# Moving the first sequence's stores and first row loads to other queues in the opening of an FFT, mixing and FFN kernel

## The chip, the cores and the metric

The kernel runs on one core of a Trainium2 chip. The core has five engines with queues of their own: TensorE (PE: matmuls; PEld: its weight loads), VectorE (DVE), ScalarE (ACT), GpSimd (POOL) and SyncE (SP, which only issues transfers here). Transfers (DMAs) run on 16 DMA engines, which SP's, ACT's and POOL's queues feed. The metric is device microseconds of one execution; less is better.

## The reference

Eight sequences of 3008 rows with 256 columns in float32 go through a real FFT along the sequence, a complex 256 x 256 mixing with bias, a soft threshold of 0.01, the inverse FFT, and then, as 24064 tokens, through a gated feed-forward block of width 1536:

```python
X = np.fft.rfft(x, axis=1)
Yr = Xr @ w_r - Xi @ w_i + b_r
Yi = Xr @ w_i + Xi @ w_r + b_i
Yr = np.sign(Yr) * np.maximum(np.abs(Yr) - lam, 0.0)
Yi = np.sign(Yi) * np.maximum(np.abs(Yi) - lam, 0.0)
y = np.fft.irfft(Y, n=x.shape[1], axis=1)
...
gate = 1.0 / (1.0 + np.exp(-(x @ w_gate)))
val = x @ w_val
return (gate * val @ w_out).astype(np.float32)
```

## The kernel before

3008 is 47 x 64. The FFT of a sequence is made in two stages with a transposition through device memory between them. The **first stage** (47 points) works on "units": `load_a(b, h)` loads unit h of sequence b (96 partitions x 4 x 256 floats, 384 KB) into a tile xf, `fwd_a(b, h)` (L178) makes two float32 products with the table `fa_sb` (`product_a`, L173) and copies each from its bank of PSUM back into xf, the first with ACT and the second with DVE for the sequences 0 and 1 (L184). `store_a(b, h)` (L186) stores the unit to zd[b]. A sequence has eight units. The **second stage** (64 points) works in twelve steps q: `load_b(b, q)` (L227) reads rows of zd[b] into a tile zf (three buffers), each step needing something of all eight stores; `load_mf(q)` loads the step's table; `fwd_b(b, q)` (L232) makes the product pb, copies it to xsh with ACT, takes the rest xsl with DVE and negates halves with ACT. `mix4` (L285) is the mixing for sequence 0 with 24 matmuls (pm, L293) and the soft threshold on DVE; `inv_b` (L298) is the inverse 64-point product (pi, L305), with the table mi of `load_mi`; its copy vz is stored to vd by POOL's queue. PSUM has three banks for all this (`FFT_BANKS`), so a product waits until the bank of the product three before it is copied out.

The change lies in the opening (L853 to L920), which handles sequence 0 whole, with the first stage of sequence 1 put in between. Its order is written out by hand (`tc.manual_schedule()`): every engine takes its instructions in the order of the text. Ahead of it stand 13 warming matmuls on a zeroed tile (`keep_warm`, L827 to L832, WARM). Then SP issues nine loads (eight units of sequence 0, one of sequence 1), and for each unit of sequence 0 the products run, and SP stores the unit; units 1 to 3 of sequence 1 are loaded behind units 1, 3 and 4, and the mixing weights w_r and w_i (`load_mix`, L747) behind unit 2. Then SP issues the table of step 0, the rows of steps 0 and 1, the table of step 1, two biases (`load_bias4`), a part of the feed-forward weights (`load_part`, the tile raw, 512 KB) and the table of step 2. TensorE makes four early units of sequence 1 (EARLY), with `mix_weights` (L760; ACT and DVE) behind the second, and ten warming matmuls (WARM_Z). Then come the steps q: rows for q + 2, the table mi, two stores of sequence 1 in each of the steps 0 and 1, the products of `fwd_b` for step q, `mix4` for q - 1, `inv_b` for q - 2, and the conversion of feed-forward weights in between.

After the opening the rest of the FFTs runs between the matmuls of the feed-forward block, in an order fixed by weights; none of that is touched.

```python
for h in range(EARLY):
    fwd_a(1, h)
    if h == 1:
        wi_sb = mix_weights()
keep_warm(bank("warm"), zero[:, :P], zero, WARM_Z)
```

Of the kernel before, what the change touches and what calls it, by code (L numbers as in the profile page):

```python
# [19 lines left out]
R2, R1 = 47, 64  # L20
NK2 = 24
NQ = 2 * NK2
# [10 lines left out]

LAST_GAP, SIDE_GAP = 20, 3
PRE = 2
WARM = 13
WARM_Z, WARM_V = 10, 5
EARLY = 4
AT_FIRST = 3
NCONV = 7  # L40
# [69 lines left out]
def tile_fft_mix_ffn(ctx: ExitStack, tc, x, w_r, w_i, b_r, b_i, w_one, w_out, mf, mi, mis, fa, fb, out):  # L110
    nc = tc.nc
# [29 lines left out]
    def bank(name, tag="fft", bufs=FFT_BANKS):  # L141
        return (psf if tag == "fft" else psl).tile([P, 512], F32, tag=tag, bufs=bufs, name=name)
# [10 lines left out]
    zd = [tc.dram_tile([NQ, R1, D], F32, name=f"zd{b}") for b in range(B)]  # L153
# [12 lines left out]
    def big(name):  # L166
        return p2.tile([P, 4, D], F32, tag="big", bufs=NBIG, name=name)

    def load_a(b, h):
        xf = p0.tile([P, 4, D], F32, name="xf0", bufs=R1 // 8) if b == 0 else big("xf")  # L170
        nc.sync.dma_start(xf[:XR], xv[b, h])
        held["x", b, h] = xf

    def product_a(xi, az, copy):
        pa = bank("pa")[:2 * NQ]
        nc.tensor.matmul(pa, fa_sb, xi, start=True, stop=True)  # L176
        copy(az, pa.rearrange("p (h c) -> p h c", h=2))  # L177

    def fwd_a(b, h):

        xf = held["x", b, h]
        for i in range(2):
            at = slice(2 * i, 2 * i + 2)
            product_a(xf[:2 * R2, at], xf[:2 * NQ, at], nc.vector.tensor_copy if b < 2 and i else nc.scalar.copy)  # L184

    def store_a(b, h, queue=nc.sync):  # L186
        queue.dma_start(zv[b][:, 4 * h:4 * h + 4], held.pop(("x", b, h))[:2 * NQ])
# [14 lines left out]
    def load_mf(q):  # L202
        t = p2.tile([P, 2, P], F32, name="mf_sb", bufs=NMF)
        nc.sync.dma_start(t, mf[2 * q:2 * q + 2].rearrange("q p k -> p q k"))
        return t
# [18 lines left out]
        nc.gpsimd.dma_start(md[2 * q:2 * q + 2].rearrange("q p a k -> p q a k"), t.bitcast(F32))  # L224
        kept.add(q)

    def load_b(b, q):  # L227
        zf = p2.tile([P, 2, D], F32, tag="ld", bufs=NLD, name="zf")
        nc.sync.dma_start(zf, zd[b][4 * q:4 * q + 4].rearrange("(q a) n c -> (a n) q c", q=2))
        held["z", b, q] = zf  # L230

    def fwd_b(b, q, m, full):  # L232
        zf = held.pop(("z", b, q))
        pb = bank("pb").rearrange("p (c q k) -> p c q k", c=CT, q=2)
        for i in range(2):
            for ct in range(CT):
                nc.tensor.matmul(pb[:, ct, i], zf[:, i, ct * P:(ct + 1) * P], m[:, i], start=True, stop=True)  # L237
        xh, xl = (p2.tile([P, CT, 3, 2 * R1], F32R, tag=t, name=t) for t in ("xsh", "xsl"))
        if full:

            xh, xl = (t.rearrange("p c s k -> p c (s k)").rearrange("p c (q k) -> p c q k", q=2) for t in (xh, xl))
            nc.scalar.copy(xh[:, :, :, 64:], pb)
            sub(xl[:, :, :, 64:], pb, xh[:, :, :, 64:])
            for t in (xh, xl):
                nc.scalar.mul(t[:, :, :, :64], t[:, :, :, 128:], -1.0)
        else:

            xf = p2.tile([P, CT, 3, 2, R1], F32, name="xsf", bufs=1)
            nc.scalar.copy(xf[:, :, 0:2].rearrange("p c t q k -> p c q t k"),
                           pb.rearrange("p c q (t k) -> p c q t k", t=2))  # L250
            nc.vector.tensor_add(xf[:, :, 2], xf[:, :, 0], xf[:, :, 1])
            flat = xf.rearrange("p c s q k -> p c s (q k)")
            nc.scalar.copy(xh, flat)
            sub(xl, flat, xh)
        held["xs", b, q] = xh, xl
# [490 lines left out]
    def load_mix():  # L746
        for w in (w_r, w_i):  # L747
            wf = f2k("wf")
            nc.sync.dma_start(wf, w.rearrange("(t p) d -> p t d", p=P))
            wfs.append(wf)  # L750

    def load_bias4():
        for i, v in enumerate((b_r, b_i)):
            nc.sync.dma_start(bias4[64 * i:64 * i + 64], v.rearrange("(o d) -> o d", o=1).broadcast_to([64, D]))

    def load_bias():
        for i, v in enumerate((b_r, b_i)):
            nc.sync.dma_start(bias_sb[:, i], v.rearrange("(o d) -> o d", o=1).broadcast_to([P, D]))

    def mix_weights():  # L760
        wi = p0.tile([P, CT, 2, D], F32R, tag="xf0", bufs=R1 // 8, name="wi_sb")
        nc.scalar.copy(wi[:, :, 0], wfs[1])
        sub(wi[:, :, 1], wfs[1], wi[:, :, 0])
        wd, wn = f2k("wd"), f2k("wn")
        sub(wd, wfs[1], wfs[0])
        nc.vector.scalar_tensor_tensor(wn, wfs[0], -1.0, wfs[1], op0=ALU.mult, op1=ALU.subtract)
        for i, w in enumerate((wfs[0], wd, wn)):
            nc.scalar.copy(w_sb[:, :, 0, i], w)
            sub(w_sb[:, :, 1, i], w, w_sb[:, :, 0, i])
        return wi  # L770
# [24 lines left out]
    def load_part():  # L795
        k, f = parts.pop(0)
        if len(parts) >= 3 * NF // 2 - NCONV:
            raw = p0.tile([P, 2, D, 2], U32, tag="xf0", bufs=R1 // 8, name="raw0")
        else:
            raw = p2.tile([P, 2, D, 2], U32, tag="big", bufs=NBIG, name="raw")  # L800
        nc.sync.dma_start(raw.rearrange("p i n w -> p (i n w)"), (w_out[f // 2] if k else w_one[f]).bitcast(U32))
        raws.append((k, f, raw))
# [12 lines left out]
    def ops(names, i):  # L815

        for n in names.split() if -len(started) <= i < len(started) else ():
            started[i].pop(n)()
        if names.endswith("lo"):
            started[:] = [t for t in started if t]  # L820
# [6 lines left out]
    def keep_warm(o, l, r, n):  # L827

        for _ in range(n):
            nc.tensor.matmul(o, l, r, start=True, stop=True)  # L830

    keep_warm(bank("warm"), zero[:, :P], zero, WARM)  # L832
    tables = {}
# [5 lines left out]
    mfs, mis_ = {}, {}  # L839
# [13 lines left out]
    with tc.manual_schedule():  # L853
        for h in range(na):
            load_a(0, h)
        load_a(1, 0)
        for h in range(na):
            fwd_a(0, h)
            store_a(0, h)
            if h in (1, 3, 4):  # L860
                load_a(1, {1: 1, 3: 2, 4: 3}[h])
            if h == 2:
                load_mix()
        mfs[0] = load_mf(0)
        for q in range(2):
            load_b(0, q)
        mfs[1] = load_mf(1)
        load_bias4()
        load_part()
        mfs[2] = load_mf(2)  # L870
        for h in range(EARLY):
            fwd_a(1, h)
            if h == 1:
                wi_sb = mix_weights()
        keep_warm(bank("warm"), zero[:, :P], zero, WARM_Z)
        for q in range(NP + 2):
            if q + 2 < NP:
                load_b(0, q + 2)
            if 0 <= q - 1 < NP:
                mis_[q - 1] = load_mi(q - 1, True)  # L880
            if q < 2:
                for h in range(q * EARLY // 2, (q + 1) * EARLY // 2):
                    store_a(1, h)
            if q == 3:
                nc.sync.dma_start(fb_sb, fb)
                load_bias()
            if q % 2 and q <= NP:
                load_part()
            if q % 2 == 0 and 4 <= q < 4 + 2 * (na - EARLY):
                load_a(1, EARLY + q // 2 - 2)  # L890
            if q < NP:
                fwd_b(0, q, mfs[q], True)
            if q + 3 < NP:
                mfs[q + 3] = load_mf(q + 3)

            if q % 2:
                ops("sum word", 0)
                start_part(p0)
                ops("exp top", -1)
            elif q:  # L900
                ops("power mant", -1)
                if len(started) > 1:
                    ops("hi lo", 0)
                ops("one", -1)
            if q == 4:
                sub(bias_sb[:, 1], bias_sb[:, 1], bias_sb[:, 0])
            if 0 <= q - 1 < NP:
                mix4(0, q - 1)
            if q == NP + 1:

                fwd_a(1, EARLY)
                store_a(1, EARLY, nc.gpsimd)
            if 0 <= q - 2 < NP:
                inv_b(0, q - 2, mis_[q - 2], True)

        for bh in beside[:NR2K]:
            load_half(*bh)
        left = ["hi lo", "power mant one", "sum word", "hi lo"]
        for h in range(EARLY + 1, na):
            ops(left.pop(0), 0)  # L920
            fwd_a(1, h)
            store_a(1, h, nc.gpsimd)
        ops(left.pop(0), 0)
# [46 lines left out]
    n = len(a3) // 3  # L970
# [13 lines left out]
    for j in range(NF, len(ffn)):  # L984
        c, f = divmod(j, NF)
# [46 lines left out]
    with tc.manual_schedule():  # L1032
# [16 lines left out]
        n = NPR * NH  # L1049
# [36 lines left out]
```

## Time and profile before

| | us |
|---|---|
| median of 3 runs (2822.7 to 2823.41) | 2823.06 |
| the profiled execution's own time | 2821.45 |
| its span | 2819.6 |
| TensorE busy in the span (99%) | 2802.0 |
| VectorE busy (74%) | 2082.6 |
| ScalarE busy (46%) | 1309.8 |
| GpSimd busy (25%) | 711.7 |

The profile is of one execution. All places in it are microseconds from the start of the span. A line such as L237 is that of the program. "SPq", "ACTq" and "POOLq" are the queues in which those engines issue transfers; a transfer's time is from its issue to its landing. In rows of a timeline, x40 counts records (a float32 product leaves several), and the brackets tell how long the engine had been idle just before, and for what. MB are 10^6 bytes.

### The profile page before, as it was taken

The page shows a single profiled execution, that of the slowest core. Times are in us where ns is not written, and L with a number is a line of the kernel's source. Part 1 is how long each engine was busy: PE and PEld are TensorE (multiplying, and loading weights), DVE is VectorE, ACT ScalarE, POOL GpSimd, SP SyncE. Part 2 cuts the span into 40 slices and gives each one's busy share as a digit, 9 for nine tenths or more (in the row PEclk, how much of TensorE's full clock was granted, in tenths as well). Part 3 has the DMA queues.
Part 4 walks back from the last instruction along what each step waited for, and adds up shares of the span by engine and source line. Part 5 has one row for each costly group of instructions (what it writes and reads, how often), then busy time and mean ns, then how long its engine had stood idle before and what let it go on. Part 6 is the DMA issues. An engine that isn't in the chain of part 4 may idle for free.

```text
span 2819.6 us, 38247 instructions
## 1 busy us (share of the span) xinstructions
PE 2802.0 (99%) x13896; PEld 2307.9 (82%) x13896; DVE 2082.6 (74%) x3109; ACT 1309.8 (46%) x2276; POOL 711.7 (25%) x638
## 2 busy tenths in 40 slices
PE   9999999999999999999999999999999999999999
PEld 6778888888899887888888888888888888888887
DVE  5778778667787536777777777777777777777776
ACT  4664544544455444444444444444444444444443
POOL 0211010224100002333333333333333343333321
PEclk9999999999999999999999999999999999999999
DMA  9866545656554661000000000000000000000000
GB/s 295 265 214 190 172 138 156 200 180 191 163 156 144 185 182 36 30 15 16 30 31 24 7 31 31 31 16 15 31 30 16 15 30 31 30 1 30 30 16 16
DMA packets 173469, 241.01 MB, mean 85 GB/s; under 512 B 14592, under 2 KB 124896, under 8 KB 173280
## 3 DMA queue, kind: packets, MB, share of 16 engines
q1 hardware_dynamic: 163776, 214.93, 24.9%
q0 software_dynamic: 9408, 23.60, 2.5%
q8 instruction: 110, 1.80, 0.3%
q14 instruction: 79, 0.65, 0.1%
q10 hardware_dynamic: 96, 0.04, 0.0%
HBM read 134.17 MB, written 104.33 MB: 85 GB/s over the span
## 4 chain that ended last, share of the span: by engine, by line
PE 95%; DVE 2%; DMA 2%; ACT 0%; issue 0%; SPq 0%; DVEq 0%; ACTq 0%
PE pd L653 11%; PE pc L653 11%; PE pa L653 11%; PE po L630 8%; PE po L629 8%; PE po L628 8%; PE pm L271 6%; PE pb L653 5%; PE pia L340 4%; PE pa L176 3%; PE pb L237 3%; PE pg L395 2%; PE pg L397 2%; PE po L420 2%; PE pg L396 2%; PE po L421 2%
## 5 line engine op out<-in xcount | busy, mean ns | idle before, releaser
L630 PE MATMUL po<-hl,w 128*128 128x512 f32 x912 | 362.7, 398 | 0.0
L629 PE MATMUL po<-hh,w 128*128 128x512 f32 x912 | 361.7, 397 | 0.0
L628 PE MATMUL po<-hh,w 128*128 128x512 f32 x912 | 360.9, 396 | 0.0
L712 POOL TENSOR_TENSOR c<-c,c 128x512 f32<-128x512 f32 x114 | 147.7, 1296 | 833.5 <-DVE c L708 613.4
L653 PE MATMUL pc<-s,w1h 128*128 128x512 f32 x912 | 284.1, 393 | 1.4 <-DVE v L687 1.4
L653 PE MATMUL pa<-a,w1h 128*128 128x512 f32 x912 | 284.1, 393 | 0.0
L708 DVE TENSOR_TENSOR c<-u,pc 128x512 f32<-128x512 f32 x228 | 156.7, 687 | 114.7 <-PE pc L653 106.3
L683 DVE TENSOR_TENSOR u<-u,pb 128x512 f32<-128x512 f32 x228 | 155.3, 681 | 91.1 <-PE pb L653 64.1
L600 ACT CAST hh<-v 128x512 fp32r<-128x512 f32 x114 | 70.7, 620 | 306.0 <-DVE v L693 306.0
L630 PEld LDWEIGHTS po<-hl,w 128*128 128x128 f32 x912 | 171.5, 188 | 41.9
L628 PEld LDWEIGHTS po<-hh,w 128*128 128x128 f32 x912 | 172.1, 189 | 40.9
L629 PEld LDWEIGHTS po<-hh,w 128*128 128x128 f32 x912 | 171.1, 188 | 40.7
L653 PEld LDWEIGHTS pa<-a,w1h 128*128 128x128 f32 x912 | 171.2, 188 | 40.1
L653 PEld LDWEIGHTS pc<-s,w1h 128*128 128x128 f32 x912 | 170.9, 188 | 39.5 <-DVE v L687 2.3
L604 POOL TENSOR_TENSOR hl<-c,hh 128x512 fp32r<-128x512 f32 x114 | 152.6, 1338 | 186.1 <-ACT hh L600 186.1
L271 PE MATMUL pm<-w_sb,xsh 128*128 128x256 f32 x1008 | 189.4, 288 | 1.4 <-ACT xf L177 1.1
L653 PE MATMUL pc<-s,w1l 128*128 128x512 f32 x456 | 177.6, 389 | 0.0
L653 PE MATMUL pa<-a,w1l 128*128 128x512 f32 x456 | 177.0, 388 | 0.0
L685 DVE TENSOR_TENSOR v<-u,pd 128x512 f32<-128x512 f32 x228 | 156.8, 688 | 25.0 <-DVE u L683 0.9
L714 DVE TENSOR_TENSOR u<-u,pd 128x512 f32<-128x512 f32 x228 | 156.9, 688 | 24.4 <-DVE c L708 0.9
L687 DVE TENSOR_TENSOR v<-v,pc 128x512 f32<-128x512 f32 x228 | 156.6, 687 | 24.1 <-DVE v L685 0.5
L679 ACT COPY u<-pa 128x512 f32<-128x512 f32 x228 | 133.7, 586 | 81.6 <-PE pa L653 81.6
(166 smaller groups left out, 6739.6 us busy)
## 6 DMA issues: line engine op xcount, KB each, us to landing
zf<-zd SPq DMA_DIRECT2D x96, 256.0 KB, 3.5
vf<-vd SPq DMA_DIRECT2D x128, 192.0 KB, 3.2
out_dram<-ot SPq DMA_DIRECT2D x93, 256.0 KB, 2.2
vd<-vz SPq DMA_DIRECT2D x84, 256.0 KB, 2.9
ypair<-yd SPq DMA_DIRECT2D x19, 1024.0 KB, 5.0
yd<-yf SPq DMA_DIRECT2D x103, 188.0 KB, 3.1
xf<-in_x_dram SPq DMA_DIRECT2D x48, 384.0 KB, 4.2
zd<-xf SPq DMA_DIRECT2D x44, 384.0 KB, 3.6
```

The lines of the kernel that those rows point to most:

```text
L271: nc.tensor.matmul(o, l, r, start=(i == 0), stop=(i == len(mms) - 1))
L604: sub_(hl, h, hh)
L628: nc.tensor.matmul(o, wh, hh, start=(f == 0), stop=False)
L629: nc.tensor.matmul(o, wl, hh, start=False, stop=False)
L630: nc.tensor.matmul(o, wh, hl, start=False, stop=(f == NF - 1))
L653: nc.tensor.matmul(o, l, r, start=not more and l is wh and r is xh, stop=l is wl, skip_group_check=more)
L683: add(u, u, b)
L685: add(v, u, d)
L687: add(v, v, c)
L708: add(c12, u, c)
L712: nc.gpsimd.tensor_mul(c12, g12, c12)
L714: add(u, u, d)
```

## The change

The stores of sequence 0 are issued from ACT's queue in place of SP's. For sequence 0 the copies change places: DVE takes the first product of a unit, ACT the second. Units 2 and 3 of sequence 1 are loaded behind units 4 and 6 (before: 3 and 4); the table of step 0 is loaded behind unit 5 (before: after all units). The rows of the steps 0 and 1 are loaded from POOL's queue. Three early units of sequence 1 stay ahead of the second warming; the fourth is made behind the product of step 0. Stores of sequence 1 go out one in each of the steps 0 to 3. WARM falls from 13 to 10 and WARM_Z from 10 to 5.

```diff
-WARM = 13
-WARM_Z, WARM_V = 10, 5
+WARM = 10
+WARM_Z, WARM_V = 5, 5
...
-            product_a(xf[:2 * R2, at], xf[:2 * NQ, at], nc.vector.tensor_copy if b < 2 and i else nc.scalar.copy)
+            product_a(xf[:2 * R2, at], xf[:2 * NQ, at], nc.vector.tensor_copy if b < 2 and i == b else nc.scalar.copy)
...
-    def load_b(b, q):
+    def load_b(b, q, queue=nc.sync):
         zf = p2.tile([P, 2, D], F32, tag="ld", bufs=NLD, name="zf")
-        nc.sync.dma_start(zf, zd[b][4 * q:4 * q + 4].rearrange("(q a) n c -> (a n) q c", q=2))
+        queue.dma_start(zf, zd[b][4 * q:4 * q + 4].rearrange("(q a) n c -> (a n) q c", q=2))
...
             fwd_a(0, h)
-            store_a(0, h)
-            if h in (1, 3, 4):
-                load_a(1, {1: 1, 3: 2, 4: 3}[h])
+            store_a(0, h, nc.scalar)
+            if h in (1, 4, 6):
+                load_a(1, {1: 1, 4: 2, 6: 3}[h])
             if h == 2:
                 load_mix()
-        mfs[0] = load_mf(0)
+            if h == 5:
+                mfs[0] = load_mf(0)
         for q in range(2):
-            load_b(0, q)
+            load_b(0, q, nc.gpsimd)
         mfs[1] = load_mf(1)
         load_bias4()
         load_part()
         mfs[2] = load_mf(2)
-        for h in range(EARLY):
+        for h in range(EARLY - 1):
             fwd_a(1, h)
...
-            if q < 2:
-                for h in range(q * EARLY // 2, (q + 1) * EARLY // 2):
-                    store_a(1, h)
+            if q < EARLY:
+                store_a(1, q)
...
             if q < NP:
                 fwd_b(0, q, mfs[q], True)
+            if q == 0:
+                fwd_a(1, EARLY - 1)
```

## Rows read from the trace of the kernel before

**Rows 1.** Page, engines: busy us (share of the span) x instructions.
```profile
PE 2802.0 (99%) x13896; PEld 2307.9 (82%) x13896; DVE 2082.6 (74%) x3109; ACT 1309.8 (46%) x2276; POOL 711.7 (25%) x638
```

**Rows 2.** Windows: busy of PE, PEld, DVE, ACT, POOL; clock, DMA share, GB/s.
```profile
48.00:84.00 36.00, 36.00 (x281) 35.02 (x282) 31.40 (x55) 23.60 (x44) 5.82 (x8) 1.00 0.93 271
```

**Rows 3.** TensorE's waits, first 48 us: total us, times, longest.
```profile
PE pb L237 <- DMA zf<-zd: 1.5, 1, 1.5
...
PE pb L237 <- issue: 1.0, 1, 1.0
...
PE pb L237 <- DMA mf_sb<-in_mf_dram: 0.5, 1, 0.5
PE pi L305 <- DMA mi_sb<-in_mi_dram: 0.4, 1, 0.4
```

**Rows 4.** Timeline of TensorE: start, us, what, records, idle before.
```profile
6.28 17.49 PE L176 MATMUL pa<-xf,fa_sb 94*96 94x512 f32 x40
24.27 1.93 PE L176 MATMUL pa<-xf,fa_sb 94*96 94x512 f32 x4 [0.50 <-DMA xf<-in_x_dram]
...
28.10 2.77 PE L830 MATMUL warm<-zero 128*128 128x512 f32 x10
31.88 1.13 PE L237 MATMUL pb<-mf_sb,zf 128*128 128x128 f32 x8 [1.02 <-issue]
...
38.97 1.13 PE L237 MATMUL pb<-mf_sb,zf 128*128 128x128 f32 x8 [1.52 <-DMA zf<-zd]
```

**Rows 5.** Timeline of TensorE in two short stretches, three warming matmuls each.
```profile
2.90 1.48 PE L830 MATMUL warm<-zero 128*128 128x512 f32 x3
...
28.65 0.85 PE L830 MATMUL warm<-zero 128*128 128x512 f32 x3
```

**Rows 6.** Chain that ended last, first 60 us: start, us, what.
```profile
21.47 7.49 DMA zd<-xf
...
32.83 6.00 DMA zf<-zd
...
49.00 0.89 PE pb L237 x8
49.89 2.84 PE pm L293 x24
```

**Rows 7.** SP's waits, first 110 us: total us, times, longest.
```profile
SPq L171 <- DMA fa_sb<-in_fa_dram: 1.9, 1, 1.9
```

**Rows 8.** Timeline of SP's queue: issues of stores 3 and 4.
```profile
16.29 0.33 SPq L187 DMA_DIRECT2D zd<-xf  x1
...
17.95 0.31 SPq L187 DMA_DIRECT2D zd<-xf  x1
```

**Rows 9.** Timeline of ACT and of DVE: an issue, copies.
```profile
0.74 0.55 ACTq L151 DMA_DIRECT2D fa_sb<-in_fa_dram  x1
...
9.05 0.58 ACT L177 COPY xf<-pa 96x512 f32<-96x512 f32 x1 [1.14 <-PE pa L176]
...
8.19 0.69 DVE L177 COPY xf<-pa 96x512 f32<-96x512 f32 x1 [6.78 <-PE pa L176]
```

**Rows 10.** Transfers, first 60 us in 40 slices of 1.5 us.
```profile
GB/s 0 143 313 278 265 262 262 262 262 262 355 407 355 377 421 366 366 415 323 11 231 246 90 200 374 400 380 379 385 371 332 330 185 167 308 358 313 302 311 386
```

**Rows 11.** Issues from 5.5, 29.45, 44, 49 and 90 us: KB, us to landing.
```profile
xf<-in_x_dram SPq DMA_DIRECT2D x2, 384.0 KB, 10.7
...
zf<-zd SPq DMA_DIRECT2D x1, 256.0 KB, 3.1
...
vd<-vz POOLq DMA_DIRECT2D x1, 256.0 KB, 5.3
...
vd<-vz POOLq DMA_DIRECT2D x1, 256.0 KB, 7.7
...
vd<-vz POOLq DMA_DIRECT2D x1, 256.0 KB, 2.6
```

## The prediction

> **What bounds the kernel now.** I read the page first: TensorE is busy 2802.0 of 2819.6 us [rows 1], so only what TensorE waits for, or what is put there to fill a wait, can be won. Then the table by stretch: from 48 us to 84 us it is busy throughout, at a granted clock of 1.00 [rows 2], so whatever the first 48 us save moves all that follows. Then TensorE's waits: the larger ones of the opening are 1.5, 1.0, 0.5 and 0.4 us, all before the 64-point products of the first sequence (pb) or the inverse ones (pi) [rows 3]. Then its timeline: ten units of the first stage in one piece of 40 records from 6.28 us, one each 1.72 us (ACT's copy of 0.58 and its idle time of 1.14 [rows 9]), ten warming matmuls from 28.10, the first pb group at 31.88, the third at 38.97 [rows 4]. Last the chain: a store zd<-xf is on its way for 7.49 us and lands at 28.96, and a row load zf<-zd is on its way for 6.00 us to 38.83 [rows 6]. So the opening is bound by a round trip: the eighth store lands, then the rows are read back. Filler stands on TensorE because of that.
>
> All this lies within the first 40 of 2820 us. The runs' median, 2823.06, lies 1.61 above the profiled execution's own time of 2821.45 and 3.46 above its span. I take differences within the trace and set them against the median. 0.2% is 5.6 us, about what a measurement of this kernel can tell from no change.
>
> **Two facts about the queues, from rows.** SP's load issue waited 1.9 us for fa_sb, a transfer that ACT had issued [rows 7]. No data ties the two. fa_sb is the first hardware transfer and xf(0,7) the ninth: each transfer waits for the one eight before it, and both hardware queues share that count. Store 3 shows it: its copies are over about 14.0 us (8.88, the end of the first DVE copy [rows 9], and three units of 1.72), but SP issues it at 16.29 [rows 8], when xf(0,7), issued near 5.6 and 10.7 us on its way [rows 11], lands. Second, the rate: slices of 1.5 us show 262 GB/s while only loads flow, and 323 to 421 from 15 us on, with loads and stores mixed [rows 10].
>
> **WARM 13 to 10.** The first warming matmuls start 0.43 us apart (the 1.48 us of three, less the 0.62 of one, over two); those before the first pb 0.23 apart (0.85 less 0.39, over two) [rows 5]. The ratio is that of the two clock levels, 1.2 and 2.4 GHz. The three removed run at the end of the thirteen, mostly at the fast pitch: 3 x 0.23 = 0.7 us; at the slow one 1.3. I take 0.7, because the slow rows end near 5 us: units start at about 5.6. TensorE does not wait for this now, so by itself it only lets stores start earlier.
>
> **Stores of the first sequence on ACT's queue.** Per unit ACT gets one issue, 0.55 us [rows 9], beside one copy of 0.58; the idle time before a copy is 1.14, so it fits. With the copies swapped ACT makes the second one and issues behind itself; DVE's is done by then. Store 0 leaves about 0.9 us earlier. But stores keep their place in the count: store 3 waits for xf(0,7), now on ACT, store 4 for xf(1,0). Behind them in ACT stand the copies of units 4 and on; with three PSUM banks TensorE stalls some 1 to 2 us. That is paid before the round trip and not on it, so I cost it at nothing while TensorE is done before the rows arrive. Landing of the eighth store, from 28.95:
> - stores 0 to 2 flow beside loads from 9.5 to 15.5 us: at 380 GB/s (middle of the mixed slices) instead of 262, 0.71 MB more, 1.9 us at 380;
> - xf(1,3) and mf0 (0.39 + 0.13 MB) may land behind it, as they are in the other queue: 1.4 us at 380;
> - against it, mf1 and the short bias now go ahead of it (0.26 MB, 0.7 us), and part of raw: 0.4 us, estimated;
> - against it, while stores 3 and 4 wait on ACT, some 3 us fall back to 262: 0.35 MB, 0.9 us.
>
> Sum -1.3, so about 27.7. Ends: 28.95 and a little over if nothing overtakes (29.7 if half of raw, 0.26 MB, is ahead); 25.5 if neither of the last two items costs anything and mf1 and the bias stay behind.
>
> What speaks against: under load a single 256 KB store in POOL's queue took 5.3 to 7.7 us to land, 2.6 in a calm stretch [rows 11], so a queue of one's own is no free lane. The Trainium skill, "DMA: Bandwidth & Descriptors", section "Issuing engines are not separate DMA queues", says that DMAs of all engines share the same 16 DMA engines and that issuing from several saves only issue time. By that rule the landing stays at 28.95; it stands below as a rival.
>
> **Rows of steps 0 and 1 on POOL's queue.** Now the second zf takes 3.1 us on SP [rows 11], and the first pb starts 2.9 us after 28.96. A POOL transfer of this size, in the other direction, took 2.6 to 7.7 [rows 11]. In the calm state that I expect it is nearest to 2.6 to 3.1; the third step's rows and store (1,0), on SP, now share the engines: I take 3.5. POOL has nothing behind these two until its first vd store near 44.7. SP's own wait for the eighth store moves from zf 0 to zf 2; mf1, the biases, raw and mf2 pass it, so the 0.5 us wait for mf goes, and zf 2, issued at 32.83 now [rows 6], leaves right behind the eighth store. It was the largest wait, 1.5 us; it goes.
>
> **The fourth early unit behind the first pb; WARM_Z 10 to 5.** No work is added; 1.72 us move into the round trip's tail, where TensorE waited for mf and zf 2. Five warming matmuls less are 5 x 0.23 = 1.2 us. Its two copies fall behind xsh and xsl of step 0 on ACT and DVE, beside TensorE's next 0.89 us; nothing. The first pb is at T; then unit 1.72, pb 0.89, pm 2.84 [rows 6]. So the third pb is at T + 0.89 + 1.72 + 0.89 + 2.84 = T + 6.34, against 38.97. Break-even is T = 32.6.
>
> **The rest.** x(1,1) stays at its place, x(1,2) and x(1,3) come a unit or two later, but ahead of their use. Stores of the second sequence leave one per step: less to share early. Both cost nothing: no wait of rows 3 is theirs.
>
> **Sum.** T = 27.7 + 3.5 = 31.2; third pb at 37.5; 1.4 us won, and 0.1 of the 0.4 us pi wait, as mi is queued earlier. 2823.06 - 1.5 = **2821.6**. Its own range, with landing 27 to 28.5 and 3.1 to 3.8 us to the first pb: 2820.4 to 2822.6.
>
> **Rivals.**
> - *The transfers are the bound anyway*: ACT's stores wait for the same earlier transfers and the engines move the same bytes, so the change does not do what it says. Landing 28.95, T = 32.45, third pb 38.8: 0.2 won, **2822.9**. For it: the shared count, store 3. Against it: the 262 GB/s slices.
> - *The stores overtake*: landing 25.5, T = 29.0, third pb at 35.3, 3.6 won, and the 0.4 of pi: **2819.1**. For it: separate queues. Against it: the slow vd stores. The same page, "Queues, rings and completion order", has each DMA engine take turns between queues by packet, which would favour this; no run here shows two hardware queues busy together.
> - *Slower: the pair on POOL's queue lands late.* Place: TensorE's wait before the first pb. zf moves in short pieces beside the larger ones of raw and store (1,0); in the loaded stretch POOL's transfers took up to 7.7 us, middle 6.5. T = 34.2, third pb 40.5, 1.5 lost: **2824.6**. It decides once landing to pb exceeds 4.9 us (32.6 less 27.7). For it: the loaded rows. Against it: that stretch had eight transfers under way.
> - *Slower: TensorE's clock falls in the longer wait.* the third early unit needs x(1,2), for which TensorE waits until 24.27 now [rows 4]; with 1.72 and 1.2 of warming TensorE is done near 27.2 and idles to 31.2, nearly 4 us against 1.0 now [rows 3]. The ten slow matmuls at the start cost 10 x (0.43 - 0.23) = 2.0 us; 1.5 won less 2.0: **2823.6**. Against it: the clock held through 1.5 us of idling [rows 3], the longest I can show. The Trainium skill, "TensorE: Matmul & The Clock Gate", section "HAM oscillation — how this bites in real kernels", says waits for DMA between bursts can throttle the clock; no run here shows it.
>
> **How the numbers follow.** Forecast 0.42, bound anyway 0.20, overtaking 0.14, late pair 0.13, clock 0.11. 80% range: from just under overtaking to just over the late pair, 2818.9 to 2824.9; what is left out is a late pair together with a clock fall (2826.6), or a still larger gain. Faster by over 0.2% needs 5.6 us: all waits in rows 3 (3.4 us) and both shortened fillers (1.9) together give 5.3, so 0.02. Slower by over 0.2%: only if two mishaps add up, 0.03. Same: 0.95.
>
> **What would show it.** Stores 0 to 7 on ACT's queue, with ACT waiting some us before stores 3 and 4; the eighth landing near 27.7; rates over 300 in the slices from 9 to 15 us; the first pb near 31.2 after a wait of 3 to 4 us; the unit behind it; no wait before the second and third pb; pitches of the first records unchanged. I am wrong in the step on the stores if the landing stays at 29, in the step on POOL if zf takes over 4.9 us, and in the clock if the first pb records are twice as long. If TensorE's busy time outside the first 100 us changes, the premise that the rest only moves is wrong.

## The result and the profile after

The changed kernel takes 2832.39 us (median of 6 runs, 2830.88 to 2834.79); the kernel before, run beside it, 2822.93 (6 runs, 2822.62 to 2823.55). The ratio is 1.0033 with a 95% interval of 1.0023 to 1.0043: 9.5 us slower, outside the predicted range and with the other sign. The profiled execution of the changed kernel took 2834.79, the longest of the six; its span is 2833.0.

The page's line of the engines, which answers to [rows 1]:

```profile
PE 2808.9 (99%) x13888; PEld 2309.3 (82%) x13888; DVE 2081.9 (73%) x3109; ACT 1309.8 (46%) x2276; POOL 712.1 (25%) x640
```

TensorE is busy 6.9 us longer with eight matmuls fewer, and idle 2833.0 - 2808.9 = 24.1 us in place of 17.6. So about half of the 13.4 us between the spans is work that ran slower, and half is waiting. The timeline of TensorE's opening shows both, to be laid beside [rows 4] (start, us, what, records, idle before):

```profile
5.90 16.87 PE L176 MATMUL pa<-xf,fa_sb 94*96 94x512 f32 x36
23.55 1.96 PE L176 MATMUL pa<-xf,fa_sb 94*96 94x512 f32 x4 [0.78 <-DVE xf L177]
26.28 3.73 PE L176 MATMUL pa<-xf,fa_sb 94*96 94x512 f32 x4 [0.78 <-DVE xf L177]
29.02 3.12 PE L830 MATMUL warm<-zero 128*128 128x512 f32 x5
37.82 2.05 PE L237 MATMUL pb<-mf_sb,zf 128*128 128x128 f32 x8 [5.68 <-issue]
39.66 3.62 PE L176 MATMUL pa<-xf,fa_sb 94*96 94x512 f32 x4
43.08 1.91 PE L237 MATMUL pb<-mf_sb,zf 128*128 128x128 f32 x8
48.48 1.05 PE L237 MATMUL pb<-mf_sb,zf 128*128 128x128 f32 x8
```

The first pb stands at 37.82 in place of 31.88, behind 5.7 us of waiting; the third at 48.48 in place of 38.97, 9.5 later. A unit of four records takes 1.96 us at 23.55 and 3.73 at 26.28; a pb group 2.05 and 1.91 until 45, then 1.05. The windows give the clock (columns as in [rows 2]: stretch, its length, then busy us of PE, PEld, DVE, ACT, POOL, and behind them the granted clock, DMA share, GB/s):

```profile
24.00:26.00 2.00, 1.50 (x4) 0.33 (x2) 0.46 (x1) 0.00 (x0) 0.00 (x0) 1.00 1.05 405
26.00:28.00 2.00, 1.72 (x2) 0.68 (x3) 0.23 (x1) 1.46 (x3) 0.00 (x0) 0.55 1.14 317
32.00:37.00 5.00, 0.14 (x1) 0.00 (x0) 0.45 (x1) 0.00 (x0) 1.64 (x2) 0.50 0.71 225
40.00:46.00 6.00, 6.00 (x18) 3.83 (x17) 1.73 (x3) 2.79 (x6) 0.00 (x0) 0.50 0.76 227
48.00:52.00 4.00, 4.00 (x37) 4.00 (x36) 3.22 (x6) 1.42 (x3) 0.00 (x0) 1.00 0.64 205
```

The granted clock is at its lower level, 1.2 GHz (0.50), from 26 to 46 us. It fell before the long wait began, right behind two idle pieces of 0.78 us in the units.

The profiled execution is the costliest of the six. The record has each execution's mean granted clock: 0.996 for this one (2834.79), 0.997 for the next slowest (2834.12), and 0.998 to 0.999 for the four from 2830.88 to 2833.24. So the others stood at the lower level for less time; where, a mean does not tell.

Next the stores. The first three leave at 8.50, 10.26 and 12.14. In the transfers of 8.5 to 13.6 us one hardware queue is at work, SP's (q1; packets, MB, share of 16 engines); ACT's (q10) has no packet there, and 276 beside 216 of SP's from 13.5 to 18 us:

```profile
q1 hardware_dynamic: 358, 1.27, 103.8%
```

The last ones in the timeline of ACT, which now issues them (stores 5, 6 and 7, counted from 0, and what ACT does beside them):

```profile
20.04 0.31 ACTq L187 DMA_DIRECT2D zd<-xf  x1
...
21.60 0.31 ACTq L187 DMA_DIRECT2D zd<-xf  x1
22.01 0.58 ACT L177 COPY xf<-pa 96x512 f32<-96x512 f32 x1 [0.98 <-PE pa L176]
26.13 0.31 ACTq L187 DMA_DIRECT2D zd<-xf  x1
26.54 1.07 ACT L177 COPY xf<-pa 96x512 f32<-96x512 f32 x2 [3.95 <-DVE xf L177]
```

The copy of the eighth unit is over at 22.59, yet its store, store 7, leaves at 26.13. The transfers in a window of 0.2 us at 20 us (store 5) say what it waited for:

```profile
zd<-xf ACTq DMA_DIRECT2D x1, 384.0 KB, 6.0
```

Store 5, issued at 20.04, is 6.0 us on its way: it lands at 26.0, and store 7 leaves 0.1 us later. By the shared count of eight, seven transfers then lie between those two. SP's timeline has six of them:

```profile
19.07 0.37 SPq L204 DMA_DIRECT2D mf_sb<-in_mf_dram  x1
20.92 0.33 SPq L171 DMA_DIRECT2D xf<-in_x_dram  x1
22.41 0.37 SPq L204 DMA_DIRECT2D mf_sb<-in_mf_dram  x1
24.18 0.56 SPq L754 DMA_DIRECT2D bias<-in_b_r_dram  x1
24.78 0.59 SPq L754 DMA_DIRECT2D bias<-in_b_i_dram  x1
25.61 0.39 SPq L801 DMA_DIRECT2D raw<-in_w_one_dram  x1
...
32.01 0.37 SPq L229 DMA_DIRECT2D zf<-zd  x1
```

mf0, x(1,3), mf1, two biases and raw: with store 6 on ACT these are the seven. In the trace stores 5 and 7 signal the same semaphore, which is what the count is made of. The last four leave ahead of store 7 because SP no longer stops at the rows of step 0. The order of the count is neither that of issue (mf0 leaves before store 5 and is counted behind it: mf2 leaves at 27.40, when mf0, 8.3 us on its way, has landed) nor that of the text (there mf1, the biases and raw stand behind store 7). Store 7, on its way for 5.9 us, lands at 32.0 (28.96 before [rows 6]); SP's zf of step 2 leaves at 32.01, at that moment. POOL's two take another 5.8 us to the first pb (POOL's timeline, then the transfers of 8 to 40 us: KB, us to landing):

```profile
32.57 1.64 POOL L229 DMA_DIRECT2D zf<-zd  x2 [32.13 <-DMA zd<-xf]
```

```profile
zf<-zd POOLq DMA_DIRECT2D x2, 256.0 KB, 5.1
...
zf<-zd SPq DMA_DIRECT2D x1, 256.0 KB, 2.7
```

The transfer of the same size that SP issued in the same microsecond took 2.7 us, POOL's 5.1. From 32.57 to 35.2 us none of the packets is of POOL's queue; its 160 packets all run from 35.2 to 38 us, when SP's are nearly over (14 packets). A smaller loss comes later: DVE's addition of a bias waits 0.98 us, and with it the next pm (DVE's and TensorE's timelines); the kernel before has no such wait:

```profile
62.77 0.43 DVE L908 TENSOR_TENSOR bias_sb<-bias_sb 128x256 f32<-128x256 f32 x1 [0.98 <-DMA bias_sb<-in_b_i_dram]
```

```profile
63.94 0.48 PE L293 MATMUL pm<-w_sb,xsh 128*128 128x256 f32 x2 [0.62 <-ACT xsh L242]
```

Each matmul behind the opening, paired with the same one of the kernel before by line and order, starts 10.0 us later from 60 to 90 us, 11.4 at 300, 12.5 at 800 and 13.2 at the end of these two executions. So 10 of the 13 us are lost in the first 60, and 3 in pieces of 0.2 to 0.7 behind them.

### The profile page after: what moved, and what is told of

Same layout as the page of the kernel before. It is cut to its first block, busy times and chain, and to the rows that moved or that the text cites. A ratio compares the mean times of both kernels' runs of the same rounds, so it can differ in the third digit from the quotient of the medians.

```text
span 2833.0 us, 38231 instructions
## 1 busy us (share of the span) xinstructions
PE 2808.9 (99%) x13888; PEld 2309.3 (82%) x13888; DVE 2081.9 (73%) x3109; ACT 1309.8 (46%) x2276; POOL 712.1 (25%) x640
## 4 chain that ended last, share of the span: by engine, by line
PE 92%; DVE 3%; DMA 1%; ACT 1%; issue 1%; SPq 0%; POOL 0%; DVEq 0%; ACTq 0%; POOLq 0%
PE pd L653 11%; PE pc L653 11%; PE pa L653 11%; PE po L630 8%; PE po L629 7%; PE po L628 7%; PE pm L271 5%; PE pb L653 5%; PE pia L340 4%; PE pa L176 3%; PE pb L237 3%; PE pg L395 2%; PE pg L397 2%; PE po L420 2%; PE po L421 2%; PE pg L396 2%
```

## The experiments

The kernel before was run beside each set: 2822.62 us beside the first four kernels, 2822.86 beside the next four, 2821.89 beside the last four (medians of 29, 29 and 33 runs). Ratios are to those. "Before +" and "after +" name the kernel that is edited.

**1. ACT's queue alone** (before +):

```diff
-            store_a(0, h)
+            store_a(0, h, nc.scalar)
```

> The kernel before with only the eight stores of sequence 0 moved to ACT's queue (old order of loads, old copies, rows on SP). Theory (count of eight): the harm in the changed kernel is not ACT's queue but what its stores wait for; here store 7 waits for w_r as before, so the stores leave about when they did and the eighth lands at 27 to 29.5 us; 2821 to 2823.5. Rival (ACT's queue itself): copies held up behind waiting issues make the eighth store leave and land 3 us late, near 32; 2826 or more, with a lower clock.

2823.57 us, ratio 1.0001 (0.9992 to 1.0010): no difference. The chain of waits has the eighth store, and TensorE's timeline the first two pb:

```profile
23.21 5.83 DMA zd<-xf
```

```profile
32.63 1.05 PE L237 MATMUL pb<-mf_sb,zf 128*128 128x128 f32 x8
34.77 1.13 PE L237 MATMUL pb<-mf_sb,zf 128*128 128x128 f32 x8 [1.08 <-DMA mf_sb<-in_mf_dram]
```

It lands at 29.04, 28.96 before. ACT's queue is no faster lane and does no harm. The units come 1.88 us apart here and in the changed kernel, 1.72 before. Here the store stands on ACT behind ACT's copy (over at 8.50) and waits for DVE's until 9.55, which holds up ACT's next copy. In the change that is not so: ACT's copy is over at 8.47 and the store leaves at 8.50.

**2. POOL's rows alone** (before +, with the new argument of `load_b`):

```diff
-            load_b(0, q)
+            load_b(0, q, nc.gpsimd)
```

> The kernel before with only the rows of steps 0 and 1 loaded from POOL's queue. Theory (POOL's landing): the first pb starts 5 to 6 us after the eighth store has landed, not 2.9, near 34.5; what SP now issues early takes the waits for mf and for the rows of step 2 away (2.0 us), so the third pb is near 39.4: 2823.5, and 2825 to 2828 if the clock falls in the longer wait. Rival (POOL as fast as SP): first pb near 32, third near 37: 2821.

2827.41 us, ratio 1.0015 (1.0005 to 1.0024): 4.8 us slower. POOL's and TensorE's timelines:

```profile
29.81 1.65 POOL L229 DMA_DIRECT2D zf<-zd  x2 [29.36 <-DMA bias<-in_b_i_dram]
```

```profile
37.01 3.38 PE L237 MATMUL pb<-mf_sb,zf 128*128 128x128 f32 x16 [5.89 <-issue]
```

7.2 us from POOL's issue to the first pb, where SP's two needed 2.9 from the landing; the third pb stands at 43.26, 4.3 later. Until 33.5 us, 3.7 us behind the issue, only packets of SP's queue run (347 GB/s); POOL's follow, and in the last 1.5 us the slices show under 150 GB/s. So POOL's loads end with the engines nearly empty but begin beside a busy SP queue: how much of the price is POOL's own and how much comes from SP's transfers is not separated here. The clock falls as well (a window of TensorE), so the 4.8 us are not POOL's alone:

```profile
38.00:40.00 2.00, 2.00 (x12) 2.00 (x12) 0.29 (x1) 0.88 (x2) 0.00 (x0) 0.54 0.03 8
```

**3. Rows back on SP** (after +):

```diff
-            load_b(0, q, nc.gpsimd)
+            load_b(0, q)
```

> The changed kernel with the rows of steps 0 and 1 issued by SP again. Theory (POOL's landing cost 2.4 to 2.9 us): eighth store still near 32, first pb near 35, third pb near 45.5; 2829.5. Rival (the rows are late because the engines are busy, whoever issues them): first pb near 37.5, 2832.

2824.99 us, ratio 1.0006 (0.9997 to 1.0015): some 7 of the 9.5 us are gone. ACT's timeline, the chain and TensorE's timeline:

```profile
22.32 0.31 ACTq L187 DMA_DIRECT2D zd<-xf  x1
```

```profile
22.32 5.85 DMA zd<-xf
```

```profile
31.10 1.13 PE L237 MATMUL pb<-mf_sb,zf 128*128 128x128 f32 x8 [1.49 <-issue]
...
37.97 1.13 PE L237 MATMUL pb<-mf_sb,zf 128*128 128x128 f32 x8 [0.29 <-DMA zf<-zd]
```

With the rows on SP nothing slips in ahead of store 7: it leaves at 22.32 and lands at 28.17, not near 32 as I had expected; pb stands 2.93 us behind it; the clock stays at full in the profiled execution. The third pb is 1.0 us earlier than in the kernel before, close to what I had predicted for the whole change, and still the time is no better. At 70 us 0.4 of that is left, and between 110 and 150 us it is lost; there TensorE's waits have one that the kernel before has not:

```profile
PE pa L176 <- DMA xfh<-in_x_dram: 1.1, 2, 0.5
```

**4. The wait filled** (after +):

```diff
-WARM = 10
-WARM_Z, WARM_V = 5, 5
+WARM = 13
+WARM_Z, WARM_V = 34, 5
```

> The changed kernel with 13 and 34 warming matmuls in place of 10 and 5, so that TensorE works through the wait for the rows. Theory (clock): the transfers land as in the changed kernel, the first pb starts near 37.8, but the pb, unit and pm records behind it run at the fast pitch, third pb near 44.2 in place of 48.5; 2828. Rival (the slow records are not the clock's, or the clock stays low): no gain, 2832 or, where the filler runs over the landing, more.

2830.57 us, ratio 1.0028 (1.0017 to 1.0038), some 1.5 us better than the change. TensorE's timeline:

```profile
27.88 8.29 PE L830 MATMUL warm<-zero 128*128 128x512 f32 x34
36.62 1.13 PE L237 MATMUL pb<-mf_sb,zf 128*128 128x128 f32 x8 [0.45 <-issue]
...
43.04 1.05 PE L237 MATMUL pb<-mf_sb,zf 128*128 128x128 f32 x8
```

Store 7 leaves at 26.18, nearly as in the changed kernel, at full clock: the clock is not what holds the store. (The warming has also moved the count: here store 7 shares its semaphore with mf0, which left at 18.87 and was 7.2 us on its way; store 5 lands only at 28.3.) From the first pb to the third it takes 6.42 us at full clock (predicted: 6.34), 10.66 in the profiled execution of the change: the clock cost 4.2 us there. The 1.5 us between the medians are not clear of noise (the two intervals overlap), and they are not the price of the fall: the mean granted clock is 1.000 in only two of the eight executions (2827.70, the profiled one, and 2828.35), 0.998 to 0.999 in the six from 2829.76 to 2833.05. The two lie 4.0 and 4.7 us under the median of the change.

**5. Only the count mended** (after +; the rows stay on POOL):

```diff
+        load_b(0, 2)
         mfs[1] = load_mf(1)
         load_bias4()
...
-            if q + 2 < NP:
+            if q and q + 2 < NP:
                 load_b(0, q + 2)
```

> The changed kernel with the rows of step 2 issued by SP ahead of mf1, the biases, raw and mf2, so that SP waits for the eighth store and those five no longer stand between stores 6 and 7 in the count of eight; the rows of steps 0 and 1 stay on POOL's queue. Theory (count): store 7 now waits for w_r and leaves near 22.3 us, not 26.1; the eighth store lands near 28.2, not 32; the first pb, still with POOL's landing of 5 to 6 us, near 34; 2828 to 2829. Rival (the eighth store is late because stores share the engines with SP's loads, whatever it waits for): landing still 31 or more, 2831 to 2833.

2829.65 us, ratio 1.0025 (1.0015 to 1.0036). ACT's, POOL's and TensorE's timelines:

```profile
22.89 0.31 ACTq L187 DMA_DIRECT2D zd<-xf  x1
```

```profile
30.49 1.65 POOL L229 DMA_DIRECT2D zf<-zd  x2 [30.04 <-DMA zd<-xf]
```

```profile
35.84 2.05 PE L237 MATMUL pb<-mf_sb,zf 128*128 128x128 f32 x8 [5.75 <-issue]
```

A load that itself waits for store 7 stops SP, nothing is counted in between, and store 7 leaves at 22.89 in place of 26.13. That is the count, shown without any other change of ACT's work. Most of the loss stays: POOL's price (5.9 us from the landing at 29.9 to pb; its first packets run 1.7 us behind its issue) and the clock (0.50 from 36 us). The 2.7 us between this median and that of the change are not clear of noise: the two intervals overlap.

**6. Rows on SP, copies as before** (after +):

```diff
-            load_b(0, q, nc.gpsimd)
+            load_b(0, q)
...
-            product_a(xf[:2 * R2, at], xf[:2 * NQ, at], nc.vector.tensor_copy if b < 2 and i == b else nc.scalar.copy)
+            product_a(xf[:2 * R2, at], xf[:2 * NQ, at], nc.vector.tensor_copy if b < 2 and i else nc.scalar.copy)
```

> The changed kernel with the rows of steps 0 and 1 on SP and ACT making the first copy of a unit again, DVE the second. Theory (copies): a product waits for the copy of the product two before it, so with DVE on the first copy a unit takes 1.88 us and with ACT 1.72; the first eight units end 1 us sooner. But the first pb follows the eighth store, so at most 0.5 us reach the end beside rows_back_on_sp: 2824 to 2825. Rival (units are slower because loads share the engines with stores): units still at 1.88.

2824.65 us, ratio 1.0006 (0.9997 to 1.0015), as experiment 3. The stores still leave 1.87 us apart. With the copies in the old order the store waits on ACT for DVE's copy, as in experiment 1, and that is enough to stretch the units. In the change the store does not wait for a copy, so what stretches them there (DVE's longer copy coming first is one candidate) stays open. In the profiled execution the clock is at 0.57 and 0.58 from 34 to 38 us, and the third pb stands at 40.89. It falls again, to 0.72 in the mean of 110 to 115 us, as it does in experiment 5's profile (0.83 there); the kernel before has 1.00.

**7. The fourth unit alone** (before +):

```diff
-        for h in range(EARLY):
+        for h in range(EARLY - 1):
             fwd_a(1, h)
...
                 fwd_b(0, q, mfs[q], True)
+            if q == 0:
+                fwd_a(1, EARLY - 1)
```

> The kernel before with only the fourth early unit moved behind the first pb. Theory: the unit fills the wait for mf (0.5 us) and 1.2 of the wait for the rows of step 2, the first pb does not move as it follows the eighth store, so the third pb, bound by the landing of its rows at 38.8, stays where it is: 2822 to 2823, no change. Rival (TensorE's work ahead of the first pb counts): 1.7 us won, 2821.

2822.43 us, ratio 0.9997 (0.9989 to 1.0006): no difference, though in the profiled execution the clock fell in the wait of 3.07 us before pb and the third pb stood at 41.23, 2.3 later. The mean clock is 0.999 in ten of the eleven executions, the profiled one among them, so the fall is likely to be in nearly all of them.

**8. The small loads ahead of the rows** (before +):

```diff
-        for q in range(2):
-            load_b(0, q)
         mfs[1] = load_mf(1)
         load_bias4()
+        for q in range(3):
+            load_b(0, q)
         load_part()
...
-            if q + 2 < NP:
+            if q and q + 2 < NP:
                 load_b(0, q + 2)
```

> The kernel before with the table of step 1 and the two short biases issued ahead of the rows, and the rows of step 2 issued right behind those of steps 0 and 1, ahead of raw; nothing else. Theory: the waits for mf (0.5 us) and for the rows of step 2 (1.5 us) go, the third pb starts at 36.6 to 37.2 in place of 39.0: 2820.5 to 2821. Rival (the rows land later because three loads share the engines, or the tables delay the eighth store): no change, 2822.6.

2821.11 us, ratio 0.9995 (0.9986 to 1.0004): the largest gain of the study, and too small to be told from none. TensorE's timeline:

```profile
32.23 2.02 PE L237 MATMUL pb<-mf_sb,zf 128*128 128x128 f32 x16 [1.20 <-issue]
...
37.95 1.13 PE L237 MATMUL pb<-mf_sb,zf 128*128 128x128 f32 x8 [0.23 <-DMA mf_sb<-in_mf_dram]
```

The waits for zf and mf of [rows 3], 1.5 and 0.5 us, go or shrink to 0.2 with a change of SP's order alone; the wait of 1.0 before the first pb stays (1.20). That is 1.0 us at the third pb.

**9. Rows back, TensorE filled** (after +):

```diff
-WARM = 10
-WARM_Z, WARM_V = 5, 5
+WARM = 13
+WARM_Z, WARM_V = 18, 5
...
-            load_b(0, q, nc.gpsimd)
+            load_b(0, q)
```

> The changed kernel with the rows of the first two steps issued by SP again, and with TensorE filled: 13 unit products ahead of the first unit again, and 18 of 128 columns in the wait for the rows. My theory has the loss of the change in three pieces: the sixteen-block price of POOL's issue, the store whose place in the count waits for another store's landing, and the clock that falls in the wait. With rows on SP the first two are gone (that kernel alone took 2825.0 by its median, and its profiled opening was 1.0 us ahead of the kernel before at the third step); what is left above the kernel before is executions in which the clock falls. Filled, TensorE has no idle stretch long enough in any of them: the granted clock stays at full from 10 us to the third step, its first product stands at 37.5 to 38.2 us, and the time is that of the kernel before or a little under, 2822.0 to 2823.5. Rival: what is left is not the clock but the later order (the bias behind sequence 1's stores, one store per step): then the time stays at 2825, and the third step's place is the same as without the filling.

2825.97 us, ratio 1.0016 (1.0007 to 1.0025): no better than experiment 3. In the profiled execution the clock is 1.00 throughout and the first units start late, at 7.17, behind warming matmuls that took 5.91 us. The filling did not keep the clock up in every execution: the two slowest (2829.72 and 2830.05) have a mean of 0.998. But the seven with 1.000 still have a median of 2824.67, 2.8 us above the kernel before. So the clock is not all that is left, and my theory of that rest falls.

**10. The same, stores of sequence 1 in pairs** (kernel 9 +):

```diff
-            if q < EARLY:
-                store_a(1, q)
+            if q == 0:
+                for h in range(2):
+                    store_a(1, h)
+            if q == 1:
+                for h in range(2, EARLY):
+                    store_a(1, h)
```

> The kernel before this one (rows on SP, TensorE filled), and the four early stores of sequence 1 put back two by two into the first two steps, where the kernel before had them, in place of one per step. In the changed kernel the first product with the point matrix waited 0.6 to 0.7 us near 54 to 64 us, behind VectorE's addition of a bias that SP had issued behind a store of sequence 1. By my theory that wait is gone, the first pm product stands 0.6 to 0.7 us nearer to the third step's pb, and the time is 0.7 us under that of the kernel with one store per step (2821.5 to 2823). Rival: the stores of the first two steps come back in front of the loads that these steps need, and the 0.7 us returns as a wait for mi or zf: no difference between the two.

2823.51 us, ratio 1.0007 (0.9998 to 1.0015): 2.5 us under kernel 9 by the medians, though the two intervals overlap; seven executions of each have a mean clock of 1.000, and the medians of those are 1.3 us apart (2824.67 and 2823.41). That is more than the 0.7 expected, and not for the reason given: DVE's addition still waits 0.50 us for a bias, and from 60 to 110 us the two kernels stand alike (1.5 and 1.3 us behind the kernel before). The difference arises later: 2.9 and 2.0 us behind at the end of the profiled executions. So one store per step seems to cost some 1 us; where its pieces come from I can't say, and the rest of what kernel 9 lost is not in it.

**11. No filler in the wait** (before +):

```diff
-WARM_Z, WARM_V = 10, 5
+WARM_Z, WARM_V = 1, 5
```

> The kernel before, with one small product in place of ten in the wait for the first rows; nothing else. It asks what the clock's fall costs by itself in the opening, with stores, rows and fourth unit as they were. Two theories of the clock: (a) the long wait itself lets it fall: TensorE is idle about 3.8 us ahead of the first pb, the granted clock of the stretch behind it is 0.5 to 0.7, the third step's first pb moves from 38.97 to 41 or 42, and the time is 2 to 3 us above the kernel before, 2825 to 2826; (b) a wait of 4 us behind four units at full clock is too short for that: the clock stays at full, the third pb stays at 39, and the time is that of the kernel before within 0.5 us.

2821.82 us, ratio 1.0000 (0.9991 to 1.0009). TensorE's timeline and a window:

```profile
32.28 4.17 PE L237 MATMUL pb<-mf_sb,zf 128*128 128x128 f32 x16 [3.41 <-DMA zf<-zd]
...
40.08 1.05 PE L237 MATMUL pb<-mf_sb,zf 128*128 128x128 f32 x8
```

```profile
34.00:36.00 2.00, 1.92 (x9) 1.65 (x9) 0.69 (x1) 1.29 (x3) 0.00 (x0) 0.50 0.59 115
```

The clock falls, as theory (a) says, with 7.80 us from the first pb to the third; yet the time is the same, as (b) says (mean clock 0.999 in ten of eleven executions, the profiled one among them). The third pb is 1.1 us late, at 70 us only 0.5 of that is left and at 200 nothing: in the kernel before TensorE waited there for other things anyway (mi at 47.90, 0.37 us), and a later opening only takes those waits' place.

**12. All small loads early** (kernel 8, and mf2 and the first mi ahead of raw):

```diff
-        load_part()
         mfs[2] = load_mf(2)
+        mis_[0] = load_mi(0, True)
+        load_part()
...
-            if 0 <= q - 1 < NP:
+            if 1 <= q - 1 < NP:
```

> An opening written from what the runs so far showed, on the kernel before: the three small loads that the first steps need (mf1, mf2 and the first mi) and the bias go ahead of or right behind the rows of the first three steps, and the raw part of the input behind them. The kernel with only mf1 and the bias ahead and the third rows right behind took 2821.1 and still showed waits of 0.23 us for mf and 0.39 us for mi. By my theory both are gone, the third pb stands at 37.5 to 37.8 us, and the time is 0.5 us under that kernel: 2820.5, or 2 us under the kernel before. Rival: the transfers' bytes are the bound, what goes ahead pushes the raw part back, and the first vd store or the first product that needs it waits as much later: no difference from 2821.1. A third possibility is that the scatter between runs, some 2 us here, covers either.

2820.98 us, ratio 0.9998 (0.9990 to 1.0007); kernel 8 had 0.9995. No difference from it, and 0.9 us under the kernel before, within the scatter. In the profiled execution, one of its slower ones (2822.05), the third pb stood at 41.24 and not at 37.5 to 37.8: the clock was at 0.50 from 26 to 34 us, behind a wait of TensorE of 1.47 us. The waits for mf and mi are gone as expected. No version beats the kernel before by more than can be measured.

## Why the prediction was wrong

By its own steps:

- **Landing of the eighth store, "about 27.7": wrong, 32.0.** "Stores keep their place in the count" was right, and I followed it for stores 3 and 4 only. The count goes over both queues, in an order of its own. I had seen that "mf1, the biases, raw and mf2 pass it" (SP's wait) and priced them by their bytes, "0.7 us" and "0.4 us". They cost places in the count: store 7 waits for store 5 (experiments 3 and 5 take it away in two ways: 22.32 and 22.89 in place of 26.13). Against the forecast 4.3 us.
- **What the two queues win, "1.9" and "1.4": not there.** With nothing but ACT's queue changed the landing is 29.04, the bound that I had kept for a rival. The term wanted over 300 GB/s from 9 to 15 us; the slices from 9 to 13.5 us show 246 to 259, no more than the 262 before, though stores 0, 1 and 2 had left at 8.50, 10.26 and 12.14. None of their bytes moved until 13.6 us, while SP's loads ran: a queue of their own did not let the stores in. From 13.5 to 18 us both queues move, at 390 GB/s (341 before). The Trainium skill, "DMA: Bandwidth & Descriptors", section "Issuing engines are not separate DMA queues", would have left the landing at 28.95; experiment 1, with 29.04, agrees.
- **"I take 3.5" for POOL's rows: wrong, 5.8 in the change, 5.9 in experiment 5 and 7.8 in experiment 2.** The rival was nearer (34.2 less 27.7 is 6.5), and the price is past its point, "once landing to pb exceeds 4.9 us". I took the price from SP's row and from a calm stretch; the loaded rows of the same queue in [rows 11] were the nearer ones. That is 2.3 us in the change; alone, with the fall of the clock that comes with it, it makes a kernel 4.8 us slower.
- **The clock as a rival of its own, 0.11: it came with the others.** A fallen clock was priced at 2.0 us. The change has 10.66 - 6.42 = 4.2 between the first pb and the third, since the fourth unit runs slow there too; experiment 7, with the same unit, has 9.24. It also fell earlier than I said, at 26 us, right behind gaps in the units: stalls of TensorE there were the right worry, but paid "before the round trip and not on it" was not the whole price. The Trainium skill, "TensorE: Matmul & The Clock Gate", section "HAM oscillation — how this bites in real kernels", has waits for DMA throttle the clock; experiments 7 and 11 show it, at 0.50.
- **Mishaps taken as alternatives.** Sum at the third pb: 4.3 (landing) + 2.3 (POOL) + 4.3 (clock) - 1.4 (the gain) = 9.5 us; 48.48 - 38.97 is 9.5. The late landing makes the wait longer, and the clock is low behind it: in the change it was down before the wait, in experiments 7 and 11 it fell within it. "a late pair together with a clock fall (2826.6)" was seen and left out of the range.
- **WARM 13 to 10, "0.7 us":** units start at 5.90, 0.4 earlier; the table fa_sb lands then (TensorE's loader waits 0.5 us for it). Other executions with 13 start at 5.86 to 7.17, so this start varies by more than the edit.
- **"The rest only moves": nearly.** 10.0 us at 60 us became 13.2 in the profiled executions. Shifts of 4 us and more travelled; smaller ones not reliably: 1.0 us won at the third pb was gone at the end in experiment 3, 0.7 of 1.0 was left in experiment 8, and 1.1 us lost was gone in experiment 11.

Right were: T + 6.34 (6.42 at full clock), the third pb near 37.5 once rows are on SP (37.97), no wait before the second pb, mf's 0.5 us gone, and the fourth unit for nothing (experiment 7). The break-even at T = 32.6 was not tested by itself.

How the 9.5 us divide by medians, each against its own kernel before: rows back on SP take off 7.1 (9.5 less 2.4), and that is clear of noise. The parts are rougher. POOL's rows cost up to 4.8 (experiment 2, with a fall of the clock in it). The count is worth some 2.7 (experiment 5: 9.5 less 6.8) and the filling 1.5 (experiment 4); both have intervals that overlap that of the change, so that the traces show these two mechanisms and the medians do not fix their size. They overlap and don't add up exactly. What stays with the rows on SP, some 2.4 us and itself hardly clear of noise, was not found and stays open: the one store per step may be a part of it (experiments 9 and 10), and later falls of the clock, such as those near 110 us in the profiles of experiments 5 and 6, another.

## What to carry to other kernels

Where transfers of several queues share a count of completions, a transfer that is moved changes which earlier one every later transfer waits for: neither the text nor the order of issue gives the count, so look in the trace, for each critical transfer, for the earlier one whose landing its issue follows. An issue on another engine's queue has that queue's price from issue to landing; take it from rows of that queue, and from loaded ones. A longer wait of TensorE is to be costed with the slower clock behind it, as one case and not as two.

## What was not expected of the hardware

- Two loads of 256 KB issued by POOL took 5.1 to 7.0 us to land, where one of SP's took 2.7 in the changed kernel and 3.1 in [rows 11]. Their first packets ran 1.7 to 3.7 us behind the issue.
- Stores in ACT's queue moved no packet from 8.5 to 13.6 us while loads of SP's queue ran at 249 GB/s.
- The granted clock fell to 0.50 behind two idle pieces of only 0.78 us in the changed kernel's profile; in the profiles of experiments 3 and 4 the same two pieces stand within 0.3 us of that place and the clock stayed at 1.00. So these pieces alone do not decide it.
- A fall of the clock in the opening left the third pb 1.1 us late and cost nothing in the whole (experiment 11): by 200 us the later waits had taken up the difference.
